# Linear attention with decay plus a squared-ReLU MLP on one core: 32 keys of the masked scores join the state product, and every engine's order is written out

## The chip, the core and the metric

The kernel runs on one core of one Trainium2 chip. A core has five engines that run side by side, each taking its own instructions in the order in which they were issued: TensorE (PE in the profile; its weight loads are PEld), VectorE (DVE), ScalarE (ACT), GpSimd (POOL) and SyncE (SP, which here only issues DMAs). The metric is the time of one execution on the device in microseconds, as a median of the runs shown.

## The reference

The attention block is a linear recurrence with a complex decay for each of 4 sequences, 8 heads, 768 steps and 48 dimensions. Its result, laid out as 3072 tokens by 384 features, goes through an MLP with 2048 hidden units. All of it is float32.

```python
for t in range(S):
    ar, ai = (a_re_n[:, :, t, :, None], a_im_n[:, :, t, :, None])
    new_re = ar * S_re - ai * S_im
    new_im = ar * S_im + ai * S_re
    kv = np.einsum('bhd,bhe->bhde', k[:, :, t], v[:, :, t])
    S_re, S_im = (new_re + kv, new_im)
    y[:, :, t] = np.einsum('bhd,bhde->bhe', q[:, :, t], S_re)
...
h = x @ w_in
r = np.maximum(h, 0.0)
g = r * r
return (g @ w_out).astype(np.float32)
```

`a_re_n` and `a_im_n` are the decays, scaled so that their magnitude stays below 0.999. The inputs `w_in` and `w_out` reach the core as 64-bit floats and are turned into float32 on the core.

## The kernel before

The 3072 tokens are cut into six units of 512 tokens, n = 0 to 5 in the code (`NU`, `L`); the change's "from unit 2 on" is n >= 1. A sequence has 768 tokens, so units 0 and 3 begin with a sequence, units 1 and 4 hold the end of one and the start of the next (`cross`; the new sequence starts at chunk 2), and units 2 and 5 end one. A unit has four chunks of 128 tokens (`C`, index j), and its eight heads are worked as four pairs (index i, two heads h each).

For each unit the work runs in four stages. `load` fetches decays, q, k and v. `chain` computes the running products of the decays over the unit, mostly on VectorE, some on ScalarE, and ends with `apply`, which multiplies q and k by those products. `pairs` is the attention proper. `dense` and `seven` (in the last unit `eleven` and `seven`) are the MLP: wide matmuls that fill TensorE for most of the time. The attention of one unit runs among the MLP matmuls of the unit before.

In `pairs`, for each pair of heads:

- `turn` or `turn_pe` writes the transposed q and k to the tile `QT`, real and imaginary part under each other: 96 of the 128 partitions. Unit 0 and three pairs of unit 1 are turned on TensorE with copies on ScalarE, the rest by VectorE transposes and DMAs from SyncE and ScalarE.
- `score` (one step for each head) multiplies k by q: up to 128 keys on the partitions, 128 queries in the columns, for four chunks into a PSUM bank. In odd chunks the two halves of the keys stand exchanged. A VectorE multiplication by `mask4` clears what a query must not see and writes the result to one of four tiles `A`, `xn`, `e`.
- `gather` brings the scaled k into token order (tile `KC`) by DMAs, and `keep` multiplies it by v: the new part of the state of each chunk. VectorE adds it up in the tile `St` (within the unit) and `S` (from unit to unit).
- `mix` multiplies, for each chunk and head, the masked scores by v (128 keys deep, 128 columns), and then, if the chunk has a state from before, adds the state by q (96 rows deep, 128 columns). In a chunk that begins a sequence the second product is left out. The two heads of a pair write different halves of the PSUM partitions of the bank `yp`. ScalarE copies the bank to `yt`, and DMAs take it to `xT`, the MLP's input.

`rows` writes the MLP's result from the tile `ot` to memory by two GpSimd DMAs for each 128 tokens. Within a chunk the tokens of a unit are kept in the order `(o c t)`: two blocks of 64 tokens, in each the tokens with equal remainder by 4 beside each other.

No instruction is issued where its code stands. Every operation is first a step of a `Plan`: engine, estimated duration, keys that it reads and writes, function, rank. `Plan.order` plays the steps through on a model of the engines and sorts them by the start that it finds; in the kernel before, each engine takes, of the steps that are ready, the one with the lowest rank, where `SHIFTS` moves the rank of some steps by hand and some rules hold small and wide matmuls together. `emit` then issues all of it in that order, so the order on every engine, the DMA queues of SyncE, ScalarE and GpSimd among them, is fixed before the kernel runs. Weights are fetched as 64-bit values by `fetch` and turned to float32 by `convert` (two ScalarE passes L947 and L952, and two or three VectorE passes L954 to L961) in the first 125 us.

Of the kernel before, what the change touches and what calls it, by code (L numbers as in the profile page):

```python
# [481 lines left out]
class Plan:  # L482
# [3 lines left out]
    MARGIN = 0.3  # L486
    SLACK = 1.7
# [6 lines left out]
    SETTLED, GROUP = 90.0, 8  # L494
    HOLD, URGENT, FILL = {"DVE": 0.15, "ACT": 0.8}, (2, 0.2), (2, 0.2)
    DRAIN = {"DVE": 0.12, "ACT": 0.13}
    SHIFTS = {
        -1193.0: (320,),
        -802.0: (1256,),
        -595.0: (2284,),  # L500
        -594.0: (2285,),
        -500.0: (2041,),
        -301.0: (2694,),
        -210.0: (2688,),
        -108.0: (2690,),
        -100.0: (range(14, 17), 25, 37, 107, range(109, 111), 113, 166, 321, 344, 346, 356, 396,
            range(575, 577), 579, 625, range(1086, 1088), range(1245, 1247), 1271, 1304, 1306,
            1588, 1824, 1826, 2117, 2691, 2697, 2708, 2716,),
        100.0: (9, 11, range(20, 22), 24, 41, 104, 210, 234, 272, 279, 284, 304, 306, 314, 327,
            329, 331, 352, 354, 373, 375, 377, 379, 406, 408, range(410, 412), 417, 422, 424,  # L510
            range(431, 433), 440, range(443, 445), 448, range(452, 454), 466, 482, 496, 507, 564,
            range(681, 683), range(684, 686), 781, 783, 788, 800, 809, range(811, 814), 865, 869,
            885, 942, 1057, range(1116, 1118), 1123, 1129, 1132, 1146, 1164, range(1175, 1177),
            1188, range(1259, 1261), 1320, 1323, 1328, 1331, 1338, 1340, 1348, 1355, 1377, 1381,
            1384, 1389, 1392, 1406, 1478, 1480, 1729, 1737, 1740, 1748, 1763, 1781, 1792, 1794,
            range(1797, 1799), 1813, 1847, 1856, 1998, range(2043, 2045), 2071, 2073, 2135, 2147,
            2155, range(2163, 2165), 2180, range(2192, 2194), 2242, 2371, 2433,
            range(2445, 2447), range(2450, 2452), range(2456, 2458), 2459, 2472, 2474, 2545,
            2578, 2581, 2592, 2633,),
        189.0: (1283,),  # L520
        197.0: (2079,),
        200.0: (871,),
        292.0: (2097,),
        293.0: (2094,),
        302.0: (2233,),
        389.0: (2557,),
        503.0: (1815,),
        504.0: (1416,),
        588.0: (1405,),
        597.0: (1827,),  # L530
        602.0: (range(1665, 1668),),
        703.0: (1821,),
        793.0: (1345,),
        802.0: (2552,),
        805.0: (2616,),
        898.0: (779,),
        903.0: (378,),
        911.0: (441,),
        996.0: (2546,),
        1009.0: (1852,),  # L540
        1016.0: (831,),
        1209.0: (403, 425,),
        1516.0: (458,),
        1717.0: (484,),
        3014.0: (1380,),
        3126.0: (879,),
        3128.0: (419,),
        3315.0: (1166,),
        3422.0: (893,),
        3520.0: (1190,),  # L550
        4109.0: (27,),
        7784.0: (407,),
        9674.0: (414,),
        11185.0: (31,),
        11579.0: (35,),
        12886.0: (402,),
        12982.0: (39,),
# [30 lines left out]
    def order(self):  # L588
        steps = self.steps
        rank = [100.0 * s[4][0] + s[4][1] for s in steps]  # L590
        for shift, which in self.SHIFTS.items():
            for ns in which:
                for n in [ns] if isinstance(ns, int) else ns:
                    rank[n] += shift
        users = [[] for _ in steps]
        left = []
        for n, s in enumerate(steps):
            left.append(len(s[2]))
            for d in s[2]:
                users[d].append(n)  # L600
        engines = ("SP", "POOL", "PE", "DVE", "ACT")
        free = {e: 0.0 for e in engines}
        wait = {e: [] for e in engines}
        done, start, at = {}, {}, {}
        bus = warm = 0.0
        tiled = False

# [3 lines left out]
        def ready(n):  # L611
            e = steps[n][0]
            t = 0.0
            for d in steps[n][2]:
                same = steps[d][0] == e and steps[d][5] is None
                hop = self.HOP[steps[d][0]]
                if same:
                    hop = self.DRAIN.get(e, 0.0) if d in steps[n][7] else 0.0
                if e == "PE" and not same and done[d] > 100.0:
                    paired = steps[d][5] is not None and steps[n][6]  # L620
                    hop += self.SLACK if paired else self.MARGIN
                t = max(t, done[d] + hop)
            at[n] = t
            wait[e].append(n)

        for n in range(len(steps)):
            if not left[n]:
                ready(n)
        flown = {True: [], False: []}
        while len(start) < len(steps):  # L630
            best = None
            for e in engines:
                if not wait[e]:
                    continue
                t = max(free[e], min(at[n] for n in wait[e]))
                if best is None or t < best[0]:
                    best = (t, e)
            t, e = best
            n = min((n for n in wait[e] if at[n] <= t), key=lambda n: (rank[n], n))
            if steps[n][4] >= self.FILL and e in self.HOLD:  # L640
                m = min((m for m in wait[e] if at[m] <= t + self.HOLD[e]),
                        key=lambda m: (rank[m], m))
                if steps[m][4] < self.URGENT:
                    n, t = m, max(t, at[m])
            if e == "PE" and t > self.SETTLED:
                if small(n) and not tiled and any(
                        small(m) and t < at[m] <= t + self.GROUP for m in wait[e]):
                    m = [m for m in wait[e] if at[m] <= t and not small(m)]
                    n = min(m, key=lambda m: (rank[m], m), default=n)
                elif tiled and not small(n):  # L650
                    m = [m for m in wait[e] if at[m] <= t and small(m)]
                    n = min(m, key=lambda m: (rank[m], m), default=n)
            line = flown[e == "POOL"]
            if steps[n][5] is not None and len(line) >= self.LANES:
                if t < line[-self.LANES] + self.LANDED:
                    at[n] = line[-self.LANES] + self.LANDED
                    continue
            wait[e].remove(n)
            _, dur, _, _, _, wire, _, _ = steps[n]
            start[n] = t  # L660
            if e == "PE":
# [14 lines left out]
            for m in users[n]:  # L676
                left[m] -= 1
                if not left[m]:
                    ready(m)
# [1497 lines left out]
```

## Time and profile before

| what | value |
|---|---|
| median of 3 runs | 654.06 us (653.98 to 654.91) |
| profiled execution | 652.32 us, of which the span of the profile is 650.4 us |
| granted TensorE clock, mean | 0.991 |
| TensorE busy | 607.8 us, 93% of the span |
| VectorE busy | 585.2 us, 90% |
| ScalarE busy | 347.0 us, 53% |
| GpSimd busy | 122.0 us, 19% |
| DMA | 80.39 MB, mean 124 GB/s |

The profile is one execution recorded by the hardware. A line such as L1707 is a line of the kernel; a row of a group gives line, engine, operation, output and input tiles, shapes, the count, the time busy in all and the mean duration in ns of one, and behind the second bar the idle time of the engine just before them with what ended it. A float32 matmul stands in it as two records of the same shape. Matmuls overlap in the pipeline, so the duration of one is longer than the distance to the next; the distance between starts is what one costs in a full stream.

### The profile page before, as it was taken

The page shows a single profiled execution, that of the slowest core. Times are in us where ns is not written, and L with a number is a line of the kernel's source. Part 1 is how long each engine was busy: PE and PEld are TensorE (multiplying, and loading weights), DVE is VectorE, ACT ScalarE, POOL GpSimd, SP SyncE. Part 2 cuts the span into 40 slices and gives each one's busy share as a digit, 9 for nine tenths or more (in the row PEclk, how much of TensorE's full clock was granted, in tenths as well). Part 3 has the DMA queues.
Part 4 walks back from the last instruction along what each step waited for, and adds up shares of the span by engine and source line. Part 5 has one row for each costly group of instructions (what it writes and reads, how often), then busy time and mean ns, then how long its engine had stood idle before and what let it go on. Part 6 is the DMA issues. An engine that isn't in the chain of part 4 may idle for free.

```text
span 650.4 us, 12670 instructions
## 1 busy us (share of the span) xinstructions
PE 607.8 (93%) x4714; PEld 540.4 (83%) x4714; DVE 585.2 (90%) x1192; ACT 347.0 (53%) x635; POOL 122.0 (19%) x214
## 2 busy tenths in 40 slices
PE   0467999999999999999999999999999999999996
PEld 0356887688678988999989999989989989998996
DVE  7989999999998999998988999988998998459981
ACT  7479889888547244538353449354447442125500
POOL 7501140221100032040032030021040130051200
PEclk9979999999999999999999999999999999999999
DMA  6972787125620056452057580056370153377631
GB/s 210 298 268 50 162 220 202 42 50 147 174 53 1 1 126 163 127 156 41 7 144 176 128 182 2 13 138 177 101 183 0 26 132 92 82 240 270 213 116 30
DMA packets 55270, 80.39 MB, mean 124 GB/s; under 512 B 11392, under 2 KB 37920, under 8 KB 55200
## 3 DMA queue, kind: packets, MB, share of 16 engines
q0 software_dynamic: 15424, 42.12, 22.7%
q1 hardware_dynamic: 35168, 31.93, 19.3%
q10 hardware_dynamic: 4608, 5.44, 3.3%
q8 instruction: 39, 0.64, 0.4%
q14 instruction: 31, 0.25, 0.1%
HBM read 48.76 MB, written 4.72 MB: 82 GB/s over the span
## 4 chain that ended last, share of the span: by engine, by line
PE 72%; DVE 17%; DMA 5%; issue 2%; ACT 2%; POOL 0%; ACTq 0%; DVEq 0%; SPq 0%
PE d L1758 24%; PE d L1869 22%; PE d L1806 5%; PE sc L1645 4%; DVE f L1444 3%; PE yp L1707 3%; PE tr L1676 3%; PE yp L1711 2%; PE d L2014 2%; DMA w<-in_moe_w_in_dram 2%; PE tr L2014 2%; DVE g L1885 2%; DVE f L1509 2%; PE sc L2014 1%; DVE aq L1461 1%
## 5 line engine op out<-in xcount | busy, mean ns | idle before, releaser
L1758 PE MATMUL d<-xT,w 128*128 128x256 f32 x888 | 198.6, 380 | 1.5 <-DMA xT<-yt 1.2
L1758 PEld LDWEIGHTS d<-xT,w 128*128 128x128 f32 x888 | 167.3, 190 | 26.2 <-DMA xT<-yt 1.5
L1869 PE MATMUL d<-T,g 128*128 128x192 f32 x576 | 100.3, 329 | 0.3 <-DVE ot L1894 0.3
L1869 PEld LDWEIGHTS d<-T,g 128*128 128x128 f32 x576 | 93.6, 190 | 2.7 <-issue 1.1
L1791 ACT ACTIVATE g<-d 128x512 f32<-128x512 f32 x74 | 43.9, 593 | 69.9 <-PE d L1758 60.6
L1869 PE MATMUL d<-w,g 128*128 128x192 f32 x432 | 75.8, 328 | 0.0
L1869 PEld LDWEIGHTS d<-w,g 128*128 128x128 f32 x432 | 71.0, 190 | 1.2 <-ACT g L1791 0.2
L1824 POOL DMA_DIRECT2D out_dram<-ot x40 | 25.3, 638 | 218.4 <-DVE ot L1894 182.7
L1546 POOL DMA_DIRECT2D KC<-f x60 | 35.5, 600 | 112.2 <-DVE f L1509 82.6
L1885 DVE TENSOR_TENSOR g<-g 128x512 f32<-128x512 f32 x72 | 48.5, 684 | 7.6 <-ACT g L1792 4.4
L1792 ACT ACTIVATE g<-g 128x512 f32<-128x512 f32 x80 | 50.5, 631 | 2.5
L1444 DVE TENSOR_TENSOR f<-aq,xn 128x384 f32<-128x384 f32 (+1 forms) x72 | 46.8, 685 | 0.0
L1806 PE MATMUL d<-w,g 128*128 128x384 f32 x128 | 43.5, 489 | 0.2 <-DVE w L961 0.2
L1598 DVE STREAM_TRANSPOSE aq<-f 128x384 f32<-128x384 f32 (+1 forms) x51 | 42.2, 902 | 0.3
L1114 DVE TENSOR_TENSOR f<-aq 128x384 f32<-128x384 f32 x72 | 37.1, 552 | 0.5
L1645 PE MATMUL sc<-QT 96*64 96x64 f32 (+1 forms) x736 | 36.8, 249 | 0.5 <-ACT QT L1628 0.5
L1645 PEld LDWEIGHTS sc<-QT 96*64 96x64 f32 x736 | 34.2, 137 | 3.0 <-ACT QT L1628 1.2
L1806 PEld LDWEIGHTS d<-w,g 128*128 128x128 f32 x128 | 23.6, 190 | 15.4 <-DVE w L961 0.9
L1894 DVE TENSOR_TENSOR ot<-ot,d 128x192 f32<-128x192 f32 x70 | 23.3, 349 | 11.5 <-PE d L1869 11.2
L1475 ACT ACTIVATE f<-aq 128x768 f32<-128x768 f32 (+1 forms) x16 | 17.2, 1083 | 28.8 <-DVE aq L1461 28.7
L1037 POOL DMA_DIRECT2D v<-in_v_dram x30 | 23.2, 791 | 24.9 <-ACT f L1067 24.5
L1711 PE MATMUL yp<-QT,St 96*48 96x128 f32 x240 | 24.5, 272 | 0.0
(313 smaller groups left out, 1114.8 us busy)
## 6 DMA issues: line engine op xcount, KB each, us to landing
QT<-aq SPq DMA_DIRECT2D x136, 64.0 KB, 2.0
f<-in_moe_w_in_dram POOLq DMA_DIRECT2D x8, 768.0 KB, 8.1
f<-in_moe_w_out_dram POOLq DMA_DIRECT2D x8, 768.0 KB, 5.4
QT<-aq ACTq DMA_DIRECT2D x68, 64.0 KB, 2.3
KC<-f POOLq DMA_DIRECT2D x40, 96.0 KB, 3.4
out_dram<-ot POOLq DMA_DIRECT2D x40, 96.0 KB, 3.7
xT<-yt SPq DMA_DIRECT2D x34, 96.0 KB, 2.5
T<-in_moe_w_out_dram POOLq DMA_DIRECT2D x4, 768.0 KB, 11.0
```

Of the source, the lines that this page charges most:

```text
L1114: lambda c=c, j=j: dve.tensor_tensor(out=f[:, j], in0=a[:, :, :, c - 1], in1=a[:, j, :, c].unsqueeze(1).to_broadcast([C, 2, HH, D]), op=AL ...
L1444: lambda j=j, r=r: dve.tensor_tensor(out=f4[:, j, r], in0=a[:, r], in1=over(j), op=ALU.mult), rk)
L1546: lambda i=i, p0=p0, m=m, src=src, queue=queue: queue.dma_start(out=kc[p0:p0 + m, i], in_=src),
L1598: lambda src=src, dst=dst: dve.transpose(out=dst, in_=src), rank)
L1645: pe.matmul(sa[p0:p0 + CH, j, t0:], lhsT=T[:, j, 1, h, t0:t0 + CH], rhs=T[:, j, 0, h, t0:], start=True, stop=True)
L1711: pe.matmul(ps[64 * h:64 * h + D, j - js[0]], lhsT=at[j][:, h], rhs=T[:, j, 0, h], start=False, stop=True)
L1758: pe.matmul(ps, lhsT=w1[:, f // FP, m, ts(f % FP, C)], rhs=xT[:, n % 2, m, ts(grp, G)], start=(m == 0), stop=(m == NM - 1))
L1791: act.activation(out=o, in_=ps, func=AF.Relu)
L1792: act.activation(out=o, in_=o, func=AF.Square)
L1806: pe.matmul(ps, lhsT=gt[:, f % 2, ts(i, C)], rhs=w2[:, f], start=(f == 0), stop=(f == NF - 1))
L1869: pe.matmul(bank[b][:, 0:DH], lhsT=gsets[x][h][:, j - HW * h, r], rhs=w(j), start=first and j == 0, stop=last and j == NT - 1)
L1885: lambda: dve.tensor_tensor(out=g[:, :, o], in0=g[:, :, x0], in1=g[:, :, x1], op=op),
```

## The change

From unit n = 1 on, the state product of `mix` takes 32 keys of the chunk's own scores along. The last 32 of the 128 partitions of three tiles, empty before, are put to use. `QT` gets the masked scores of the chunk's first 32 keys for its first 32 queries (two ScalarE copies for each pair and head, two chunks each; `("q0", ...)`). `St` and `S` get the 32 rows of v that belong to those keys (two ScalarE copies for each pair, and one for each unit; `("sv", ...)`, `("Sv", ...)`). The remaining 96 columns of those rows in `QT` are kept at zero, once, by `clear` on GpSimd. The state product is then 128 rows deep and comes first; the score product follows with columns 32 to 127 alone. Every chunk now has a state product: where a sequence begins, the state is set to zero on GpSimd. For this to be right, the first 32 queries of a chunk may see only the first 32 keys, so the tokens within a chunk are ordered in four blocks of 32 in place of two of 64, which shows in `mask`, `turn`, `turn_pe`, the last unit's copies, and in `rows`, which sends four DMAs of 32 tokens in place of two of 64.

`SHIFTS` and the rules of `order` are replaced by `ORDER`: for each engine a list of numbers, each the place of a step among that engine's steps sorted by rank. The play on the model remains for the interleaving between engines. Besides, `sums` is cleared first of all on GpSimd.

```diff
-    MARGIN = 0.3
-    SLACK = 1.7
...
-    SHIFTS = {
...
+    ORDER = {
+        "SP": """
+            220-222 2 0-1 5 4 224 3 6 225 223 226 14 7 13 15 9 17 16 8 228 19 12 11 18 10 20 227
...
+        "PE": """
+            539-553 0-1 554 2-3 555-559 4-6 560 7 561-565 8 566-570 42 571-574 44-45 43 48 53 51
...
     def order(self):
         steps = self.steps
-        rank = [100.0 * s[4][0] + s[4][1] for s in steps]
...
+        line = {}
+        for e, text in self.ORDER.items():
+            own = sorted((n for n, s in enumerate(steps) if s[0] == e),
+                         key=lambda n: (steps[n][4], n))
+            line[e] = []
+            for part in text.split():
+                a, _, b = part.partition("-")
+                line[e] += own[int(a):int(b or a) + 1]
...
         while len(start) < len(steps):
...
+            heads = [(ready(e), line[e][head[e]], e) for e in line if head[e] < len(line[e])]
+            t, n, e = min(h for h in heads if h[0] is not None)
+            head[e] += 1
...
+    QC = C // 4
...
-            part = part.rearrange("p (o c t) -> p o c t", o=2, c=W)
-            pool.affine_select(out=part, in_=part, pattern=[[CH, 2], [1, W], [W, C // 8]],
+            part = part.rearrange("p (o c t) -> p o c t", o=4, c=W)
+            pool.affine_select(out=part, in_=part, pattern=[[QC, 4], [1, W], [W, C // 16]],
...
+    def clear(s, rank):
+        z = QT[s].rearrange("p (i k x) -> p i k x", i=W, k=2)[C - QC:C, :, 0]
+        keys = [("QT", s, 0), ("QT", s, 1)] + ([("t", 0), ("t", 1)] if s == 2 else [])
+        step("POOL", 0.9, [], keys, lambda: pool.memset(z, 0.0), rank)
...
+            if n == 0:
+                return
+            near = QT[s].rearrange("p (i o k h t) -> p i o k h t", i=W // 2, o=2, k=2, h=2)
+            a4 = As[a].rearrange("p (j o t) -> p j o t", o=2, t=C)
+            for o in range(2):
+                step("ACT", 0.3, AK[a], [("q0", s, h, o)], lambda o=o: act.copy(
+                    out=near[C - QC:C, :, o, 0, h, 0:QC], in_=a4[CH * o:CH * o + QC, :, o, 0:QC]),
+                    rank)
...
+            for o in range(2 if n else 0):
+                js_ = slice(0, 3, 2) if o else slice(1, 2)
+                jv = slice(1, W, 2) if o else slice(2, 3)
+                step("ACT", 0.4 if o else 0.3, [("v", vs(n))], [("sv", s, o)],
+                     lambda o=o, js_=js_, jv=jv: act.copy(
+                         out=sf[C - QC:C, js_], in_=v5[CH * o:CH * o + QC, jv, 2 * i:2 * i + 2]),
+                     rank)
+            if cross:
+                step("POOL", 0.2, [], [("st", s, 2)], lambda: pool.memset(st[:, 1], 0.0), rank)
...
-            got["S", i] = at, s
+            got["S", i] = [of, sf[:, 0], sf[:, 1], sf[:, 2]] if n else at, s
...
                     for j in js:
-                        for h in range(2):
+                        for h in range(2 if n else 0):
+                            pe.matmul(ps[64 * h:64 * h + D, j - js[0]], lhsT=at[j][:, h],
+                                      rhs=T[:, j, 0, h], start=True, stop=False)
+                        for h in range(2 if n else 0):
+                            pe.matmul(ps[64 * h:64 * h + D, j - js[0], QC:C],
+                                      lhsT=v5[:, j, 2 * i + h], rhs=aa[h][:, j, QC:C],
+                                      start=False, stop=True)
+                        for h in range(0 if n else 2):
                             pe.matmul(ps[64 * h:64 * h + D, j - js[0]], lhsT=v5[:, j, 2 * i + h],
                                       rhs=aa[h][:, j], start=True, stop=at[j] is None)
-                        for h in range(2):
+                        for h in range(0 if n else 2):
                             if at[j] is not None:
...
+        if which[0] == 0 and n:
+            Sn = Sb[n % 2]
+            if fresh:
+                step("POOL", 0.4, [], [("S", n % 2, i) for i in range(NP)],
+                     lambda: pool.memset(Sn[0:R], 0.0), rank)
+            step("ACT", ac(DM) + 0.15, [("v", vs(n))], [("Sv", n % 2)], lambda: act.copy(
+                out=Sn[C - QC:C].rearrange("p (h d) -> p h d", h=H), in_=v5[0:QC, 0]), rank)
...
-        for p0 in (0, CH):
+        for p0 in range(0, C, QC):
             dma(pool, [("ot", o, 0), ("ot", o, 1)], [], lambda p0=p0: pool.dma_start(
-                out=out[r + p0:r + p0 + CH, :].rearrange("(t c) e -> c t e", c=W),
-                in_=ots[o][p0:p0 + CH]), (DENSE, n), CH * DM * 4)
+                out=out[r + p0:r + p0 + QC, :].rearrange("(t c) e -> c t e", c=W),
+                in_=ots[o][p0:p0 + QC]), (DENSE, n), QC * DM * 4)
...
+            for s in range(3):
+                clear(s, (PAIR, 1))
```

300 lines of the change are left out of this document (161 added, 139 removed).

## The prediction

> **What bounds the kernel now.** I read the page's busy shares and chain first, then the busy time by stage, then the matmuls of one `mix` in order of time, then the chain itself, the groups by shape and the front of the timeline.
>
> ```profile
> span 650.4 us, 12670 instructions
> ...
> PE 607.8 (93%) x4714; PEld 540.4 (83%) x4714; DVE 585.2 (90%) x1192; ACT 347.0 (53%) x635; POOL 122.0 (19%) x214
> ...
> PE 72%; DVE 17%; DMA 5%; issue 2%; ACT 2%; POOL 0%; ACTq 0%; DVEq 0%; SPq 0%
> ```
> ```profile
> core 0: us, PE busy (x) PEld busy (x) DVE busy (x) ACT busy (x) POOL busy (x), PEclk, DMA share, GB/s
> 0.00:72.00 72.00, 36.59 (x353) 30.55 (x355) 65.71 (x155) 52.32 (x103) 24.59 (x62) 0.93 0.68 203
> 72.00:84.00 12.00, 11.14 (x189) 10.02 (x185) 11.93 (x23) 11.47 (x19) 0.89 (x2) 1.00 0.66 148
> 84.00:125.00 41.00, 40.41 (x164) 31.03 (x165) 40.61 (x77) 37.54 (x53) 9.15 (x13) 1.00 0.59 159
> 125.00:237.00 112.00, 112.00 (x793) 93.20 (x792) 108.39 (x247) 64.26 (x134) 20.50 (x36) 1.00 0.30 77
> 237.00:410.00 173.00, 172.88 (x1456) 158.69 (x1455) 160.74 (x334) 89.82 (x173) 28.91 (x48) 1.00 0.46 112
> 410.00:510.00 100.00, 99.45 (x782) 91.59 (x780) 91.94 (x174) 49.31 (x90) 14.89 (x22) 1.00 0.40 100
> 510.00:567.00 57.00, 56.94 (x548) 52.01 (x550) 47.08 (x78) 19.08 (x28) 7.76 (x12) 1.00 0.40 95
> 567.00:645.00 78.00, 78.00 (x441) 73.22 (x438) 58.46 (x110) 23.18 (x39) 15.32 (x21) 1.00 0.53 179
> ```
>
> The first figure after the bounds is the stretch, the second PE's busy time. From 125 us to 645 us PE idles 0.73 us in all. Before 72 us VectorE is the busy one. So the time is a front set by VectorE, plus PE's work at the granted clock 1.00, plus a tail of about 5 us behind the last matmul. ScalarE and GpSimd have room, and DMA does not set the pace.
>
> **The columns of `mix`.** These are matmuls of one `mix` in unit n = 3, in order of time (start, us, line, tiles, depth and columns, count), and stretches of the chain (start, us).
>
> ```profile
> 348.20 0.46 PE L1711 MATMUL yp<-QT,St 96*48 96x128 f32 x4
> 348.42 0.27 PE L1707 MATMUL yp<-e,v 128*48 128x128 f32 x1
> ...
> 348.64 0.46 PE L1711 MATMUL yp<-QT,St 96*48 96x128 f32 x4
> ```
> ```profile
> 254.04 1.30 PE d L1869 x8
> ...
> 369.93 1.50 PE d L1869 x8
> ...
> 379.80 20.72 PE d L1758 x96
> 400.52 5.21 PE d L1869 x32
> ```
>
> A float32 matmul is two records, and the two heads run side by side: the four state records of a chunk, 96 rows deep, take 348.42 - 348.20 = 0.22 us, and the four score records behind them, 128 deep, 348.64 - 348.42 = 0.22 us. A pair of records takes 0.110. Per record 256 columns take 20.72 / 96 = 0.216 us and 192 columns 5.21 / 32 = 0.163: 0.84 to 0.86 ns a column at all three widths, with no constant part. I take 96 columns at 0.0825 us a pair. The other end is 0.110, the row of 128 columns: nothing saved.
>
> Narrowed: 5 units x 4 pairs x 4 chunks x 2 passes = 160 pairs of records x 0.0275 = -4.4 us. Added: every chunk now needs its state matmul, since that carries 32 keys. Before, chunk 2 of n = 1 and n = 4 (a sequence starts there) and chunk 0 of n = 3 had none: 3 x 4 pairs of heads = 12 chunks x 0.22 = +2.64 us. Net -1.76 us (0 saved on columns would make it +2.64). Units 2 and 5 gain 0.88 us each, the others about nothing. The 128-row depth in place of 96 costs nothing by the equal 0.22 us above.
>
> In the Trainium skill, "TensorE: Matmul & The Clock Gate", section "Back-to-back issue gap", says that in a stream of weight loads and matmuls both set the spacing, about 81 ns at 128 columns and 131 at 512. As an estimate from that page, 32 columns would be worth 4 ns a matmul in place of 13.75, and the columns -1.3 us in place of -4.4, a net loss of 1.3. The trace does not bear that out: its spacing follows the columns.
>
> **Changes between small and wide work.** The eight L1869 records take 1.50 us behind score work and 1.30 behind wide work, 0.2 us for coming back. Counted in this trace, PE goes 76 times between the two kinds (`score`, `keep`, `mix`, against the rest). With the numbers of the written PE list put against the steps I count 64. Six returns less: -1.2 us.
>
> **The front.** Unit 0 has the same instructions; only orders differ.
>
> ```profile
> 33.96 1.88 ACT L952 ACTIVATE w<-w 128x768 f16<-128x768 int16 x1
> 34.11 0.43 DVE L1197 TENSOR_TENSOR KC<-yt 128x96 f32<-128x96 f32 x2 [0.83 <-ACT yt L1222]
> ...
> 35.89 0.30 DVE L1197 TENSOR_TENSOR KC<-yt 128x36 f32<-128x36 f32 x2 [0.34 <-ACT yt L1222]
> ...
> 38.03 0.95 DVE L961 CUSTOM_DVE_ANT_0 w<-KC,w 128x1536 uint16<-128x1536 uint16 x1
> ```
>
> VectorE waits 0.83 and 0.34 us for small ScalarE copies that stand behind weight conversions of 1.9 us. The written ScalarE list has those two conversions later, one between the two `back` copies, the other behind the second pair's `keep`. The L961 at 38.03 goes from ahead of the scan's wide products into the later part of `apply`. All three together are 2.1 us. But the VectorE work ahead of unit 0's last score mask falls by only 0.34 us, since other steps take the places. I take -1.0 us, between -2.1 and +2.1 (the same amount given back where a conversion is now too late for the wide matmuls).
>
> **ScalarE's copies.**
>
> ```profile
> L1792 ACT ACTIVATE g<-g 128x512 f32<-128x512 f32 x80 | 50.5, 631 | 2.5
> ...
> L1791 ACT ACTIVATE g<-d 128x512 f32<-128x512 f32 x74 | 43.9, 593 | 69.9 <-PE d L1758 60.6 <-issue 6.6 <-DMA QT<-aq 1.3
> ...
> L1648 DVE TENSOR_TENSOR A<-sc,mask 128x512 f32<-128x512 f32 x28 | 18.3, 681 | 1.9 <-PE sc L1645 1.9
> ...
> L1686 ACT COPY St<-tr 96x96 f32<-96x96 f32 x16 | 3.8, 234 | 7.3 <-DVE St L1690 4.1 <-PE tr L1676 1.7 <-PE yp L1711 1.4
> ...
> L1889 ACT COPY ot<-d 128x192 f32<-128x192 f32 x10 | 3.1, 312 | 21.1 <-PE d L1869 21.0
> ...
> L1386 ACT COPY car<-ce 32x24 f32<-32x24 f32 x12 | 2.5, 208 | 0.2
> ...
> L1811 ACT COPY ot<-d 128x384 f32<-128x384 f32 x4 | 1.9, 478 | 6.8 <-PE d L1806 6.8
> ```
>
> Scores: 80 copies of 64 elements x 0.22 (between 208 ns at 24 elements and 234 at 96) = 17.6 us. v: 20 of 96 x 0.234 and 20 of 192 x 0.312 = 10.9. The carried state's v: 5 of 384 x 0.478 = 2.4. Together 31 us, ScalarE 347 to 378 of 650: free as throughput. As latency it lies between the mask and `mix`: mask 0.68, then for the last head two copies of 0.22, some 1.3 us with the hops. The cover is the wide work that PE's list puts between the second score and its `mix`. Counted with the rows' 1.30 us per eight records, the least of the twenty goes from 1.30 us (three mixes) to 2.6; four are under 3.4 (fourth pair of n = 3, 4 and 5, first pair of n = 5). I take 0. Without that cover 0.4 to 0.5 us at each of 20 mixes, 8 to 10 us, would stand at PE's head, with all wide matmuls behind it. A copy that waits for its mask also holds up the relu behind it on ScalarE, and so a PSUM bank.
>
> **GpSimd and the queues.**
>
> ```profile
> L1546 POOL DMA_DIRECT2D KC<-f x60 | 35.5, 600 | 112.2 <-DVE f L1509 82.6 <-issue 13.3 <-DVE St L1690 12.1
> ...
> L1824 POOL DMA_DIRECT2D out_dram<-ot x40 | 25.3, 638 | 218.4 <-DVE ot L1894 182.7 <-ACT ot L1811 25.2 <-DVE f L1114 7.6
> ```
> ```profile
> out_dram<-ot POOLq DMA_DIRECT2D x40, 96.0 KB, 3.7
> ...
> KC<-f SPq DMA_DIRECT2D x24, 48.0 KB, 3.0
> ```
> ```profile
> 0.96 0.32 POOL L816 MEMSET mask<- 128x256 bf16 x1
> ```
>
> Output rows go in 80 issues in place of 40: 40 x 0.638 = 25.5 us on GpSimd, plus a dozen memsets of up to 1024 elements (256 take 0.32, so 1.3 us at most): 122 to about 155 us of 650. The engine idles over 260 us for VectorE, so 0. Where a row issue stands just ahead of a KC gather, the gather and the `keep` behind it come 0.64 us later. Landing hardly depends on size (3.0 at 48 KB, 3.7 at 96). SP's list has the same issues in other places: 0, within a transfer of about 3 us. The finer order of tokens (blocks of 8 for 16 in transposes and copies) keeps every size: 0, bounds -0.5 and +0.5.
>
> **The sum.** -1.76 - 1.2 - 1.0 = -3.96 us. The profiled execution took 652.32 us (650.4 of span, 1.9 around it) and would take 648.4; it lies 1.74 below the median 654.06 of three, which gives 650.1 us.
>
> **The rivals.** *The front gives all.* The 2.1 us and PE's 0.86 + 0.59 us idle between 72 and 125 us go too: -1.76 - 1.2 - 2.1 - 1.45 = -6.5, 647.5 us. For it, the three waits are real; against it, VectorE's count.
>
> *VectorE paces the middle.*
>
> ```profile
> 181.43 0.87 DVE f L1081
> ...
> 234.34 1.03 DVE aq L1598 x2
> ...
> 407.44 0.87 DVE f L1444
> ...
> 493.35 1.20 DVE KC L1360 x3
> ...
> 510.06 4.17 PE d L1869 x24
> ```
>
> The chain runs through VectorE from 181 to 235, 407 to 422 and 493 to 510 us, and VectorE is busy 108.39 of 112 us there. What PE saves earlier would then turn into waits, and only unit 5 behind 510 us counts: -0.88 and two returns, -0.4: 652.8 us. Against it, VectorE idles 12 us between 237 and 410.
>
> *The columns do not pay.* If the weight loads set the pace, +2.64 - 1.2 - 1.0 = +0.4: 654.5 us. The 0.216, 0.163 and 0.110 speak against it. The page's rule above leads this way.
>
> *Slower: the score copies come late.* Place: the four mixes with under 3.4 us of cover. Needed are 1.3 us; a relu and square ahead of the copies on ScalarE add 1.22, and a mask that waits on VectorE behind one step of 0.95 us (L961 above) takes it over 3.4. If each then stands 1.3 us: +5.2 - 3.96 = +1.2, and 655.3 us. It decides from about 1 us each, where the gain is gone.
>
> **How the numbers follow.** Forecast 0.45; the front gives all 0.15; VectorE paces 0.17; columns do not pay 0.08; copies late 0.15. About 0.2% (1.3 us) is what a measurement can tell from no change. The forecast and the first rival are faster, 0.60, and about half of VectorE's case, 0.08: 0.68. The other half, three quarters of the columns' case and a little of the late copies: 0.17 same. The rest is slower, 0.15. The forecast's own range is 648 to 652. The range for the time goes from 646.5, the first rival with the token order's -0.5 and most of PE's last 0.73 us of idle, to 654.6, the columns' case.
>
> **What would show it.** Right: L1707's successor with 128x96 in pairs 0.08 us apart; 320 state records 128 rows deep (a few may be missing); 64 changes of kind; PE busy about 3 us less; unit 0's wide matmuls starting about 1 us sooner; PE idle behind 125 us still under 1.5 us. Wrong: PE waiting for an ACT copy ahead of `mix`, for KC ahead of `keep`, or VectorE stretches in the chain that grew.

## The result, and the profile after

The changed kernel takes 649.22 us (median of 4 runs, 648.35 to 650.27), the kernel before 654.02 us beside it (652.9 to 654.91): a ratio of 0.9928, 95% interval 0.9907 to 0.9949. That is 4.8 us or 0.7%, outside the 0.2% that a measurement can tell. Run again on another occasion it was 649.64 us against 654.84, ratio 0.9917 (0.9886 to 0.9949). The forecast was 650.1.

The page of the changed kernel's profiled execution (650.27 us), its span, busy shares and chain by engine:

```profile
span 648.1 us, 12935 instructions
...
PE 603.7 (93%) x4762; PEld 539.9 (83%) x4762; DVE 581.9 (90%) x1192; ACT 378.9 (58%) x760; POOL 149.7 (23%) x266
...
PE 86%; DVE 6%; DMA 2%; ACT 1%; issue 1%; SPq 1%; ACTq 0%; DVEq 0%
```

ScalarE goes from 347.0 to 378.9 us and GpSimd from 122.0 to 149.7; TensorE falls by 4.1 us. VectorE's part of the chain is 6% where it was 17%. The labels of lines move: L1707 is now L1765, L1711 is L1762, L1758 is L1830, L1869 is L1941.

By stage (the same columns as before; the figure behind the stretch's length is PE's busy time):

```profile
125.00:237.00 112.00, 111.70 (x807) 92.95 (x806) 110.05 (x243) 76.79 (x171) 33.01 (x54) 1.00 0.35 86
237.00:410.00 173.00, 172.51 (x1478) 159.58 (x1477) 160.97 (x332) 100.98 (x214) 39.62 (x70) 1.00 0.48 111
410.00:510.00 100.00, 100.00 (x809) 93.42 (x807) 91.61 (x177) 52.76 (x114) 18.21 (x30) 1.00 0.38 97
510.00:567.00 57.00, 57.00 (x574) 52.82 (x574) 42.60 (x73) 28.25 (x58) 11.79 (x18) 1.00 0.42 100
567.00:645.00 78.00, 74.39 (x401) 69.34 (x399) 59.61 (x113) 22.38 (x40) 17.68 (x25) 1.00 0.56 181
```

Between 125 and 567 us PE idles 0.79 us, as little as before. In the last stretch it is busy 74.39 of 78 us: it is through with its work 4 us earlier.

One chunk of a `mix` of unit n = 3 (start, us, line, tiles, depth and columns, count):

```profile
346.51 0.45 PE L1762 MATMUL yp<-QT,St 128*48 128x128 f32 x4
346.73 0.25 PE L1765 MATMUL yp<-e,v 128*48 128x96 f32 x1
...
346.89 0.45 PE L1762 MATMUL yp<-QT,St 128*48 128x128 f32 x4
```

The four state records, now 128 rows deep and first, still take 346.73 - 346.51 = 0.22 us. The four score records of 96 columns take 346.89 - 346.73 = 0.16 us.

To see where the time went, I count in the traces: the start of the first matmul record of the MLP, the start of the next one when 160 of them have started (called the 160th here), the end of the last matmul, and what the span has behind it.

| us | before | changed | changed, run again |
|---|---|---|---|
| first wide matmul starts | 80.6 | 81.1 | 81.2 |
| 160th starts | 123.3 | 123.1 | 122.7 |
| from there to the last matmul's end | 522.1 | 518.3 | 516.8 |
| behind the last matmul | 5.0 | 6.7 | 6.9 |
| span | 650.4 | 648.1 | 646.4 |

So next to nothing was gained in front (0.2 to 0.6 us at the 160th), 3.8 to 5.3 us behind 123 us, and 1.7 to 1.9 us was given back at the very end. The profiled execution of the kernel before (652.32 us) is a quick one among its runs, so the two spans lie 2.3 us apart where the medians lie 4.8; what its slower runs lose, no trace shows.

### The profile page after: what moved, and what is told of

It reads as the page before. It is cut to its first block, busy times and chain, and to the rows that moved or that the text cites. A ratio compares the mean times of both kernels' runs of the same rounds, so it can differ in the third digit from the quotient of the medians.

```text
span 648.1 us, 12935 instructions
## 1 busy us (share of the span) xinstructions
PE 603.7 (93%) x4762; PEld 539.9 (83%) x4762; DVE 581.9 (90%) x1192; ACT 378.9 (58%) x760; POOL 149.7 (23%) x266
## 4 chain that ended last, share of the span: by engine, by line
PE 86%; DVE 6%; DMA 2%; ACT 1%; issue 1%; SPq 1%; ACTq 0%; DVEq 0%
PE d L1830 30%; PE d L1941 27%; PE d L1878 6%; PE sc L1681 5%; PE tr L1730 3%; PE yp L1762 3%; PE d L2086 2%; PE yp L1765 2%; PE tr L2086 2%; PE sc L1830 2%; PE sc L2086 1%; DMA xT<-yt 1%; PE d L1660 1%; DVE f L1150 1%; PE tr L1660 1%; PE yp L2086 1%
## 5 line engine op out<-in xcount | busy, mean ns | idle before, releaser
L1830 PE MATMUL d<-xT,w 128*128 128x256 f32 x888 | 197.9, 380 | 1.0 <-DMA xT<-yt 1.0
L1830 PEld LDWEIGHTS d<-xT,w 128*128 128x128 f32 x888 | 167.7, 190 | 25.1 <-issue 2.0
L1941 PE MATMUL d<-T,g 128*128 128x192 f32 x576 | 100.6, 328 | 0.3 <-DVE g L1957 0.3
L1941 PEld LDWEIGHTS d<-T,g 128*128 128x128 f32 x576 | 94.0, 190 | 1.5 <-DVE g L1957 0.6
L1896 POOL DMA_DIRECT2D out_dram<-ot x80 | 48.5, 610 | 157.8 <-DVE ot L1966 140.0
L1941 PE MATMUL d<-w,g 128*128 128x192 f32 x432 | 76.7, 328 | 0.0
L1941 PEld LDWEIGHTS d<-w,g 128*128 128x128 f32 x432 | 71.0, 190 | 1.3 <-ACT g L1864 0.2
L1634 DVE STREAM_TRANSPOSE aq<-f 128x384 f32<-128x384 f32 (+1 forms) x51 | 44.0, 910 | 0.2
L1681 PE MATMUL sc<-QT 96*64 96x64 f32 (+1 forms) x736 | 38.6, 250 | 0.0
L1730 PEld LDWEIGHTS tr<-v,KC 128*33 128x33 f32 (+1 forms) x544 | 19.2, 126 | 4.3 <-issue 3.4
```

Of the source, the lines that this page charges most:

```text
L1634: lambda src=src, dst=dst: dve.transpose(out=dst, in_=src), rank)
L1681: pe.matmul(sa[p0:p0 + CH, j, t0:], lhsT=T[:, j, 1, h, t0:t0 + CH], rhs=T[:, j, 0, h, t0:], start=True, stop=True)
L1830: pe.matmul(ps, lhsT=w1[:, f // FP, m, ts(f % FP, C)], rhs=xT[:, n % 2, m, ts(grp, G)], start=(m == 0), stop=(m == NM - 1))
L1896: dma(pool, [("ot", o, 0), ("ot", o, 1)], [], lambda p0=p0: pool.dma_start(out=out[r + p0:r + p0 + QC, :].rearrange("(t c) e -> c t e", c= ...
L1941: pe.matmul(bank[b][:, 0:DH], lhsT=gsets[x][h][:, j - HW * h, r], rhs=w(j), start=first and j == 0, stop=last and j == NT - 1)
```

## The experiments

The kernels ran in three sets of four; in each set the kernel before ran beside them (654.84, 654.13 and 654.59 us). Intervals are those of the ratio to it. The kernel before differs by up to 0.7 us between the sets, and medians of six runs leave about 1 us open, so smaller differences between two changed kernels are not clear of the noise.

**The changed kernel again.**

> The changed kernel unaltered, as the baseline for the other kernels and to see by how much one profiled execution differs from the next. Theory (the account of the two traces): from the 160th wide matmul on PE needs 3.8 us less, the front is equal within 0.3 us, and the end behind the last matmul takes 1.75 us more (6.7 against 5.0), since the last three VectorE additions stand in another order. Then every profile of this kernel has 6.7 us behind the last matmul and 32 stretches of small work behind the 160th wide matmul, and the median is 4 to 5 us under that of the kernel before. Rival (the end's 6.7 us is chance of one execution): 5 to 6 us here.

It took 649.64 us, with 6.9 us behind the last matmul. So the longer end is no chance of one execution.

**The order alone.** The kernel before takes its steps from the written lists, each list without the steps that it does not have.

```diff
-        rank = [100.0 * s[4][0] + s[4][1] for s in steps]
...
+        for e, text in self.ORDER.items():   # the written lists, added steps left out
...
```

> The kernel before with its own arithmetic (four 128-column score products, two blocks of 64 tokens, no copies below Q and below the state), but every engine's steps in the written order, the added ones left out. Theory: the order brings two stretches of small work fewer behind 123 us (-0.4), fewer waits in wide work (-1.1), nothing in front and +1.75 at the end; so 0 to -1 us against the kernel before, about 653.5 us, and 9 to 10 us of idle at no place. Rival A (the written order brings the whole gain): -4.5 us or more, 649.5. Rival B (the columns bring it all and the order costs): 654 to 656.

654.31 us, ratio 0.9987 (0.9967 to 1.0007): no change clear of the noise, and far from rival A. The theory's 653.5 and rival B's 654 to 656 it cannot tell apart. What PE waited for most from 125 us on (line, what it waited for, us in all, times, longest):

```profile
PE sc L1666 <- DMA QT<-aq: 3.2, 2, 2.7
```

In the changed kernel this wait is absent. The written order fits the timing of the new arithmetic; to the old one it brings no gain that can be measured.

**The arithmetic alone.** The changed kernel, with the common steps in the old order.

```diff
     ORDER = {
-        "PE": """539-553 0-1 554 2-3 ...
+        "PE": """   # the order that the kernel before issued; likewise on every engine,
+                    # each added copy or memset where its inputs are ready
```

> The changed kernel's arithmetic, copies and output rows, but the steps that both kernels have stand in the order of the kernel before on every engine, and each added step stands where what it reads is ready by the model of that kernel. Theory: the columns bring -1.6 us and the end stays at 5.0, but mix now follows its score mask too closely for the two ScalarE copies (1.30 us of wide work between them at three mixes, and copies queue behind relu and square): 0.4 to 1.2 us of PE idle at most of 20 mixes, 8 to 15 us in all, so 660 to 668 us. Rival A (the cover of 1.3 us is enough, the copies cost nothing in any order): 652 us, no PE idle ahead of mix. Rival B (the columns bring all of the gain whatever the order): 649.

668.18 us, ratio 1.0192 (1.0158 to 1.0226): 13.3 us slower, just above the range. PE's longest waits from 125 us on, then ScalarE around one of them:

```profile
PE yp L1742 <- ACT QT L1673: 2.4, 3, 1.2
PE yp L1742 <- ACT yt L1764: 1.6, 1, 1.6
```
```profile
183.16 0.84 ACT L1088 ACTIVATE f<-f 128x768 f32<-128x768 f32 x1 [2.67 <-DVE f L1086]
...
185.87 0.49 ACT L1673 COPY QT<-A 32x64 f32<-32x64 f32 x2
```

The copies L1673 stand behind ScalarE work that waited 2.67 us for VectorE. ScalarE has time enough, but its instructions go in order: what counts is what stands ahead of the copy.

**The same without the score copies.** The step stays, its copies go; the first 32 queries of a chunk lose their first 32 keys.

```diff
-                step("ACT", 0.3, AK[a], [("q0", s, h, o)], lambda o=o: act.copy(
-                    out=near[C - QC:C, :, o, 0, h, 0:QC], in_=a4[CH * o:CH * o + QC, :, o, 0:QC]),
-                    rank)
+                step("ACT", 0.3, AK[a], [("q0", s, h, o)], lambda o=o: None, rank)
```

> The kernel with the changed arithmetic in the order of the kernel before (668.2 us, 13.3 more than the kernel before), again without the 80 ScalarE copies of masked scores. Theory (in that order mix stands too close behind its mask, and PE waits for these copies and for the relu behind them): most of the 13.3 us plus the 1.6 that the columns save go, so 653 to 656 us. Rival A (the other added steps where I put them, the copies of v and the memsets on GpSimd, hold up the engines): 663 to 668. Rival B (the finer order of tokens and twice the output DMAs cost it): the same, above 660, but with PE waiting for xT or for KC.

661.52 us, ratio 1.012 (1.0097 to 1.0143): still 7.4 us slower than the kernel before of its set. So the copies were about 6 of the 13.3 us (5.9 against the kernel before of each set, 6.7 by the medians alone). The theory's 653 to 656 is missed, rival A's 663 to 668 as well, but the waits are of rival A's kind and not of rival B's (`xT`, `KC`). The two longest from 80 us on that end with ScalarE's relu:

```profile
PE d L1919 <- ACT g L1842: 2.0, 1, 2.0
PE d L1919 <- ACT g L1841: 1.1, 3, 0.6
```

PE now waits for the relu (`g` from ScalarE): it seems that other added steps, in my places, hold ScalarE's queue. Which of them, no run here shows.

**The arithmetic alone, copies placed better.** The same order of the common steps, other places for the added ones.

> Again the changed arithmetic in the order of the kernel before on every engine, but the added ScalarE copies and GpSimd memsets stand in other places among the unchanged steps: chosen so that no copy stands where it holds up the relu or the copies behind it for longer than need be, and ahead of the mix that reads it. Theory (of the 13.3 us that the first such kernel lost, most was the head of ScalarE's queue waiting, in my places, and only part is mix too close behind its mask): columns -1.6, about +3 for the mixes with 1.3 us of cover, 654 to 657 us. Rival A (the short distance from score to mix is what costs, wherever the copies stand): 662 or more. Rival B (with well-placed copies the old order carries the change as well as the written one): 649 to 651.

662.64 us, ratio 1.0113 (1.0089 to 1.0137): 5.5 us better than the first placing and still 8.1 slower than the kernel before, in rival A's range. Its reason, the short distance from score to `mix`, is not all of it. Here is the worst place, `mix` of one pair on PE and the end of ScalarE's queue at that time:

```profile
359.47 0.42 PE L1741 MATMUL yp<-QT,S 128*48 128x128 f32 x2 [0.67 <-ACT QT L1672]
362.61 0.31 PE L1741 MATMUL yp<-QT,S 128*48 128x128 f32 x1 [2.72 <-ACT QT L1672]
```
```profile
361.76 0.51 ACTq L1618 DMA_DIRECT2D QT<-aq  x1
362.31 0.24 ACT L1672 COPY QT<-A 32x64 f32<-32x64 f32 x1 [2.49 <-DMA QT<-aq]
```

The fourth copy L1672 starts at 362.31. Ahead of it stands a DMA that ScalarE has to issue (L1618, at 361.76), which waits in its turn; `mix` waits 2.72 us. I did not find a placing that the old order carries; that none exists is not shown.

**The written order without the score copies.** The same edit in the changed kernel.

> The changed kernel in its written order without the 80 ScalarE copies of masked scores below Q (the rows below Q stay zero, so the first 32 queries lose their first 32 keys); the copies of v stay. It takes away 17 us of ScalarE work and the step between mask and mix. Theory (the wide work that stands between the second score and mix covers the copies): equal to the changed kernel within 0.5 us, 649.6. Rival (the copies cost on PE's path, at the four mixes with under 3.4 us of cover or by holding up the relu): -2 to -5 us.

649.37 us, ratio 0.9925 (0.9907 to 0.9943): equal to the changed kernel (649.64) within the noise. All that PE waited for behind 125 us:

```profile
PE d L1939 <- ACT g L1861: 0.3, 1, 0.3
```

In the written order the 80 copies cost nothing that can be measured.

**All 128 columns.**

```diff
-                            pe.matmul(ps[64 * h:64 * h + D, j - js[0], QC:C],
-                                      lhsT=v5[:, j, 2 * i + h], rhs=aa[h][:, j, QC:C],
+                            pe.matmul(ps[64 * h:64 * h + D, j - js[0], 0:C],
+                                      lhsT=v5[:, j, 2 * i + h], rhs=aa[h][:, j, 0:C],
```

> The changed kernel, but the score product of mix runs over all 128 columns again and not 96 (the first 32 queries of a chunk then get their first 32 keys twice). 160 pairs of records become 32 columns wider. Theory (spacing follows columns; 0.0616 us a record at 128 columns and 0.0492 at 96 by a fit over the stretches of small work): 320 x 0.0124 = +4.0 us against the changed kernel, 653.2 us. Rival (the spacing of small matmuls is set by weight loads and a constant part, 4 ns for 32 columns): 320 x 0.004 = +1.3 us, 650.5. A third (the columns are hidden by waits elsewhere): under +0.5 us.

653.27 us, ratio 0.9975 (0.9956 to 0.9993): 3.6 us over the changed kernel of the same set, give or take 1.1. From the 160th wide matmul to the last matmul's end it takes 3.9 us more than the run again and 2.4 more than the first trace of the changed kernel, which has 0.8 us of waits there. One chunk, the same place in unit n = 3:

```profile
347.72 0.45 PE L1762 MATMUL yp<-QT,St 128*48 128x128 f32 x4
347.94 0.27 PE L1765 MATMUL yp<-e,v 128*48 128x128 f32 x1
...
348.15 0.45 PE L1762 MATMUL yp<-QT,St 128*48 128x128 f32 x4
```

The chunk takes 0.43 us in place of 0.38; over 80 chunks that is about 4 us. The columns are worth most of what the prediction put on them, and the spacing follows them; the rival's 1.3 us is out.

**No state product where a sequence begins.**

```diff
+                        both = n and not (fresh if j == 0 else cross and j == 2)
-                        for h in range(2 if n else 0):
+                        for h in range(2 if both else 0):   # state product, then 96 columns
...
-                        for h in range(0 if n else 2):
+                        for h in range(0 if both else 2):   # 128 columns of scores alone
...
```

> The changed kernel, but the 12 chunks in which a sequence begins (chunk 2 of units n = 1 and 4, chunk 0 of n = 3) have no state product again; their score product runs over 128 columns. 48 records of 128 columns at 0.049 us less, 48 score records 0.0124 us longer each. Theory: -2.36 + 0.6 = -1.8 us against the changed kernel, 647.9 where the changed kernel has 649.6. Rival A (the PE time is given back at waits for VectorE in units 1, 3 and 4): 0 to -0.6. Rival B (with less PE work ahead of them the score copies and the relu are now late): slower, 650 to 651.

648.62 us, ratio 0.991 (0.9889 to 0.9931); 1.0 under the changed kernel and 0.75 under the kernel without score copies of the same set, neither clear of the noise. PE's busy time falls by 1.6 to 1.8 us (603.7 and 603.6 in the two traces of the changed kernel, 602.0 here), as the theory has it. PE's longest waits in this kernel from 80 us on:

```profile
PE d L1831 <- DMA xT<-yt: 1.9, 2, 1.3
PE sc L1681 <- DMA QT<-aq: 0.9, 2, 0.4
```

The longest, 1.3 us for `xT`, is at 86.9 us, ahead of every chunk that the edit touches (the first `mix` of n = 1 starts at 161 us), so it is not the edit's. The others, 0.9 us for `QT` and 0.5 for `xT`, lie behind; the changed kernel has 0.3 for `xT` there. So part of the 1.8 us may be given back where PE now comes to `QT` before its DMAs have landed (rival A); how much, these runs do not tell.

**The last additions.** VectorE's last three additions in the old order.

> The changed kernel with one edit: the last VectorE additions stand as in the kernel before, so that the one that waits for TensorE's last matmul comes last and ScalarE's DMA, not SyncE's, is the last to go. In two profiles of the changed kernel SyncE issues its last DMA 1.06 us after the last matmul, starts its row of waits on semaphores 3.3 us later and is through with them 1.4 us after that; 6.7 to 6.9 us from the last matmul to the end, 5.0 in the kernel before. Theory (the place of the three additions): 0.65 us from the later issue and about 1 us from SyncE's row of waits, so -1.0 to -1.7 us against the changed kernel: 648.2 us where the changed kernel has 649.6, and 5.0 to 6.0 behind the last matmul. Rival (the kernel with columns alone had the old additions and still 6.5 us: the end is set by a wait of each engine behind its last branch, different from run to run): under 0.5 us.

647.81 us, ratio 0.9908 (0.9884 to 0.9931). The end of three traces: the kernel before, the changed kernel, and this one (line, tiles, count; SPq and ACTq are DMA issues).

```profile
642.63 2.76 PE L1869 MATMUL d<-T,aq 128*128 128x192 f32 x16
...
645.43 0.35 DVE L1894 TENSOR_TENSOR ot<-ot,d 128x192 f32<-128x192 f32 x1 [2.25 <-PE d L1869]
645.82 0.38 ACTq L1818 DMA_DIRECT2D out_dram<-ot  x1
```
```profile
637.00 5.80 SPq L1890 DMA_DIRECT2D out_dram<-ot  x2
638.63 2.76 PE L1941 MATMUL d<-T,aq 128*128 128x192 f32 x16
...
641.43 1.01 DVE L1966 TENSOR_TENSOR ot<-ot,d 128x192 f32<-128x192 f32 x3 [4.46 <-PE d L1941]
641.81 0.38 ACTq L1890 DMA_DIRECT2D out_dram<-ot  x1
```
```profile
636.84 2.76 PE L1941 MATMUL d<-T,aq 128*128 128x192 f32 x16
...
639.64 0.35 DVE L1966 TENSOR_TENSOR ot<-ot,d 128x192 f32<-128x192 f32 x1 [2.25 <-PE d L1941]
640.02 0.38 ACTq L1890 DMA_DIRECT2D out_dram<-ot  x1
```

Before, one addition of 0.35 us and ScalarE's DMA follow the last matmul (642.63 + 2.76). In the changed kernel three additions of 1.01 us in all wait for it, and SyncE's last DMA goes at 642.46, after ScalarE's. With the old order of the three the span ends at 645.3, 5.7 us behind the last matmul in place of 6.7 to 6.9; over all kernels here the old order has 5.0 to 6.5, the new one 6.6 to 7.2. On the mean that is 5.7 us over the six traces with the old order and 6.9 over the eight with the new one, so about 1.1 us go with the order; the rest differs from one execution to the next. By the medians it is 1.8 us, 1.6 against the kernel without score copies of the same set; the intervals overlap, so the traces carry this more than the times.

**The front of the kernel before.**

```diff
     ORDER = {
+        # on each engine: first what the kernel before starts in its first 84 us, in its order;
+        # then the rest in the written order
```

> The changed kernel, but on each engine the steps that the kernel before starts in its first 84 us stand first and in that kernel's order; all others follow in the written order. Theory (the traces: the first wide matmul at 81.1 to 81.2 us in the changed kernel and 80.6 in the kernel before, the 160th at 122.7 to 123.1 against 123.3): the written front is worth 0 to 0.5 us, so 649.6 to 650.1. Rival A (the prediction: the front brings 1.0 us, up to 2.1): 650.6 to 651.7. Rival B (the written front costs, since TensorE waits 11 to 12 us in it for the totals and its clock is lower behind that): 648 to 649.

655.78 us, ratio 1.0003 (0.9983 to 1.0023): 6 us slower than the changed kernel, outside all three. The first wide matmul, and PE some microseconds behind it (in brackets the idle time ahead of a row and what ended it):

```profile
81.30 0.70 PE L1827 MATMUL d<-xT,w 128*128 128x256 f32 x2
```
```profile
86.29 1.03 PE L1827 MATMUL yp<-xT,w 128*128 128x256 f32 x4
90.67 2.93 PE L1827 MATMUL sc<-xT,w 128*128 128x256 f32 x6 [3.36 <-DVE w L989]
```

The front itself is as fast (81.30 us). Behind it PE waits 3.36 us for a weight that VectorE converts too late: the edges of the two orders do not fit together. So this tells nothing of the front's own worth, beyond the start of the first wide matmul.

**Twenty more round trips.** In 20 stretches of small work a wide step from beside them is put into the middle.

> The changed kernel with the same steps, but in 20 of its stretches of small work behind 125 us one wide step beside the stretch is moved into its middle: 104 changes of kind in place of 64, 20 round trips more, no work added. Theory (0.18 to 0.21 us a round trip by a fit over the stretches of two traces): +3.8 us, 653.4. Rival A (a change costs on both sides, 0.16 or more each way): +6.6, 656. Rival B (the cost of a change lies in the waits that come with it, a change alone is free): under +1, 650.5.

655.12 us, ratio 1.0008 (0.9996 to 1.0021): 5.5 us over the changed kernel, 0.27 a round trip, between the theory and rival A. PE waits for nothing behind 125 us in this trace, so rival B is out. PE in unit n = 3, where six wide records of 256 columns were put between `keep` and `score`:

```profile
339.47 1.56 PE L1831 MATMUL d<-xT,w 128*128 128x256 f32 x6
340.96 1.56 PE L1682 MATMUL sc<-QT 96*64 96x128 f32 x32
342.45 2.86 PE L1831 MATMUL d<-xT,w 128*128 128x256 f32 x12
345.15 1.46 PE L1942 MATMUL d<-w,g 128*128 128x192 f32 x8
346.45 2.75 PE L1831 MATMUL d<-xT,w 128*128 128x256 f32 x12
```

The eight records of 192 columns amid wide work take 346.45 - 345.15 = 1.30 us, 0.163 each and nothing on top. The six at 339.47 take 1.49 us where six of 0.216 make 1.29; the twelve behind `score` take 2.70 in place of 2.59. By the starts of single records, over the whole trace, the first wide record behind small work takes 0.104 us more than usual and the last one ahead of small work 0.093; from the last small record to the first wide one it is 0.15 us, where small ones start 0.02 to 0.06 apart.

**Both gains together.** No state product where a sequence begins, and the old order of the last additions.

> The changed kernel with both edits that gained alone: the last VectorE additions as in the kernel before (647.8, against 649.6 of the changed kernel), and no state product in the 12 chunks that begin a sequence (648.6). Theory (one is behind the last matmul, the other in the middle, so they add): -1.8 - 1.0 = -2.8 us, 646.8, a ratio to the kernel before near 0.988. Rival (the second gain is not there: the PE time is given back at waits for QT and xT): 647.8.

646.66 us (645.21 to 648.25), ratio 0.9878 (0.9855 to 0.9902): 7.9 us under the kernel before and about 3.0 under the changed one (2.6 under its first runs). Of the kernels here it is the fastest, and the two edits together are clear of the noise.

## Why the prediction was right, point by point

**Columns and state products (-1.76 us).** Right in mechanism, and near in size: score records of 96 columns lie 0.08 us apart in pairs, as forecast, and the 160 pairs are worth 3.6 us by the medians, give or take 1.1, where the prediction has 4.4. The added state products were costed at +2.64 against the old form. Taking them out again, with the score product of those chunks at full width, took 1.6 to 1.8 us off PE's busy time; of the kernel's time it took 1.0 us by the medians, which is not clear of the noise. By an estimate from the rule of the Trainium skill that was weighed against the rows ("TensorE: Matmul & The Clock Gate", section "Back-to-back issue gap") the wider product would have cost 1.3 us; the runs decide against it here. The same page of the Trainium skill, section "Wait — 56ns, not 53.3ns?", gives columns divided by 2.4 GHz plus 2.5 ns for one matmul; as an estimate from it 320 records one behind another are worth 4.3 us. That is near the measured size, but the formula does not describe these float32 records: at 256 columns it gives 109 ns where the trace has 216, so the nearness at 96 columns, where two records run side by side, proves nothing.

**Round trips (-1.2 us).** Right. The count of changes, 76 to 64, is found in the trace exactly: 38 returns before, 32 after. Two things were off by a little and cancel: a round trip costs 0.27 us and not 0.2, and of the six returns one lies in the first 84 us, where PE waits for VectorE anyway; behind the 160th wide matmul there are 30 before and 25 after (two of the 30 lead to transposes of `turn_pe` first). Five times 0.27 is -1.35 us.

**The front (-1.0 us).** This step failed. The first wide matmul of both kernels (before, then changed):

```profile
80.61 0.70 PE L1758 MATMUL d<-xT,w 128*128 128x256 f32 x2
```
```profile
81.08 0.70 PE L1830 MATMUL d<-xT,w 128*128 128x256 f32 x2
```

It starts 0.5 us later, not 1.0 sooner, and the 160th is 0.2 to 0.6 sooner. The two waits for `yt` that the prediction quoted are indeed gone, but VectorE waits elsewhere in the changed kernel's first 84 us (two of the rows):

```profile
DVE f L1106 <- ACT f L1098: 1.1, 1, 1.1
...
DVE A L1684 <- PE sc L1681: 0.7, 1, 0.7
```

VectorE is busy 77.64 us of the first 84 before and 77.62 after, so it idles as long as before. One more thing is different there: the clock granted to TensorE in the first 72 us is 0.88 on the mean (0.93 before). Whether that costs anything, no run here shows.

The prediction had counted that the VectorE work ahead of unit 0's last mask falls by only 0.34 us, and put 1.0 all the same. The count was nearer than the choice: a wait that goes is only a gain if nothing else is late at the same place.

**ScalarE's copies (0).** Right, and the place of the copies matters as the prediction said: without them the changed kernel is equally fast, while in the old order they cost about 6 us in the first placing. The prediction's 8 to 10 us "without that cover" was for the copies alone, so it is somewhat large; that the whole change in the old order is 8 to 13 us slower than the kernel before is another number, since over half of it (7.4 of 13.3 us) stays without the copies. And the cover is not wide PE work alone. It is also what stands ahead of the copy on ScalarE: work that waits for VectorE, and DMA issues.

**GpSimd and the queues (0).** 149.7 us busy, against "122 to about 155", and 48 KB rows land in 3.6 us; no wait of PE for `KC` appeared. It was not tested alone.

**What the sum left out.** The end behind the last matmul, +1.7 to 1.9 us between these traces; about 1.1 of it go with three additions whose order on VectorE changed, and the kernel before has the shortest end of all traces here. The prediction gave all of its attention to the order ahead of PE. On the other side PE has less to wait for: gaps over 0.12 us beyond the usual spacing sum to 1.7 us before, 1.3 and 0.5 in two traces of the changed kernel. Columns and state products by the records' mean spacing (-1.6), round trips (-1.35) and waits (-0.4 to -1.2) make -3.4 to -4.2 of the measured -3.8 to -5.3 behind 123 us. The rest, 0.4 to 1.2 us, lies in gaps too small to assign. So two of the sum's three terms hold, and that -3.96 came so close to -4.8 is partly luck: the front's -1.0 is all but absent and the end costs over 1 us, and fewer waits on PE, which the sum does not have, make up for them.

**The rivals.** VectorE does not pace the middle: its part of the chain fell from 17% to 6%. The columns pay (3.6 us), and the front does not give all, nor anything near it. The late score copies, the slower rival, are a real mechanism; this written order avoids it. Order and arithmetic cannot be costed apart: the one alone is worth -0.5 us (not clear of the noise), the other +8 to +13, both together -5.

## What to carry to other kernels

Before an engine is given small work that lies between two steps of another, look at what stands ahead of it in that engine's queue and not at its share of busy time: the same 80 copies of 0.24 us cost nothing in one order and about 6 us in another. Cost the end behind the last matmul as a stage of its own when an order is rewritten; the last instructions have no cover, and about 1 us was lost there unseen. A product that multiplies a state of zeros to keep the code uniform can be dropped for the few chunks that have none; here that took 1.6 to 1.8 us off PE's busy time, though its gain in the kernel's time is not shown by itself.

## What the runs showed of the hardware

- Going from wide to small matmuls (other row and column sizes of the tile) and back costs 0.27 us in a full stream, 5.5 us for 20. The spacing shows 0.09 us at the last wide record and 0.10 at the first after the return. The Trainium skill, "TensorEngine Tiling (Array Packing)", section "Key Properties", says that changing the tiling mode drains TensorE; it gives no figure. A cost at each of the 20 added round trips, with no wait beside it, agrees with that; that it is the drain, no run shows by itself.
- At the end of the changed kernel ScalarE, VectorE and SyncE each stand about 3 us between their last branch and their next instruction (642.22 to 645.49, 642.10 to 645.15, 642.84 to 645.87 us); SyncE then goes through twenty waits in 1.4 us. With 4.4 us of this behind SyncE's last DMA, it matters when that DMA goes: SyncE's last branch lies 1.5 us behind the last matmul in the eight traces with the new order of the additions and 1.8 us ahead of it in the six with the old. What fills the 3 us no run here tells, nor why some traces have a second stretch of that kind: VectorE in the kernel with the arithmetic alone, whose end takes 6.5 us with the old order, stands another 2.5 us (662.57 to 665.07 us).
